# A cast moved from an engine to a DMA transfer in three of 24 groups, with output products one step later

## The chip, the cores and the metric

The kernel runs on one core of a Trainium2 chip. Its time is the device time of one execution in microseconds (us); the number compared is the median of several runs. Five engines work side by side, each through its own queue in order: TensorE (PE in the rows), VectorE (DVE), ScalarE (ACT), GpSimd (POOL) and SyncE (SP), which here issues all transfers between HBM and the on-chip memory SBUF and the transposing transfers inside SBUF. Results of matrix products land in PSUM, which GpSimd and transfers don't use in this kernel.

## The reference

Three steps follow each other. First an attention: `kv` (384 x 32 positions, 128 channels) is averaged over 4 x 4 blocks to 768 keys, multiplied by `w_sr`, and serves as keys and values for 12288 queries:

```python
s = scale * (q @ k.transpose(0, 2, 1))
a = softmax(s)                      # shown in short
x = a @ v
```

Then two layers with 2048 inner features follow, with float64 weights:

```python
h = x @ w_in;  g = maximum(0.01 * h, h);               x = g @ w_out    # first layer
h = x @ w_in;  g = h if h >= 1, 0 if h <= -1, else (h + 1)**2 / 4;  out = g @ w_out
```

## The kernel before

**Groups and steps.** The 12288 tokens are cut into 24 groups of 512 columns. Each layer treats its 2048 inner features in 16 steps of 128. To keep the precision with 16-bit products, each operand is split into a high half and a low half (`..h`, `..l`), and a product of two operands is three matmuls: high by high, low by high, high by low.

**One step of the first layer** (group g, step j). `proj_in` makes three matmuls into a PSUM tile `h`. `leaky` on ScalarE applies the activation and writes `lt` in float32 (line 764). `leaky_hi` makes `gh`, a float16 copy of `lt` (line 772): on ScalarE in group 1 and on GpSimd from group 2 on (`GP = 2`). Group 0 uses float32 products and has no split. `leaky_lo` on VectorE makes `gl = lt - gh` (line 777). `proj_out` adds three matmuls into the accumulator `acc`: part 0 the two on `gh`, part 1 the one on `gl` (line 748). The tile rings hold 6 tiles of `lt` (`LT`) and 6 pairs of `gh` and `gl` (`B0`).

**One step of the second layer.** `quad_a`, `quad_s` (ScalarE), `quad_g` (VectorE), `quad_hi` (ScalarE or, in part from group 4 on, GpSimd) and `quad_lo` (VectorE) do the same for the other activation. The second layer of a group begins well after its first layer: at the start of the kernel several first layers run before any second one, and from some 170 us on the two are interleaved step by step, with the attention of a later group between them.

**Weights and attention.** In the first 100 us the weights are converted as well (lines 346 to 365 and the helpers at lines 115 and 118). The attention of each group makes four tiles of 128 queries, whose 768 weights are normalised on ScalarE and VectorE and transposed by a transfer that SP issues (line 529).

**What sets the order.** Nothing is ordered at run time but by each engine's queue. A planner inside the kernel (`op` and `run_list`) writes these queues. Each operation is entered with a wished-for step number (`when`), an engine, an estimated cost in ns (`cost`), the time after its end until others see it (`late`), the tiles that it needs and makes, and the ring that it takes a slot of. `run_list` then simulates the engines and always emits the operation that can start first, corrected by its wished-for step. Output products of the first layer have the wished-for step `b + F1 + 0.4 * p` with `F1 = 3`, where b is the step of their first products. Operations of VectorE and GpSimd that share a memory port (`port`) exclude each other in the simulation through `lock`, and a GpSimd operation that would have to wait for the lock is put back by 100 ns (line 963).

Of the kernel before, what the change touches and what calls it, by code (L numbers as in the profile page):

```python
# [20 lines left out]
POOL = 4  # L21
# [7 lines left out]
def attention_moe_kernel(  # L29
# [22 lines left out]
    nc = tc.nc  # L52
# [715 lines left out]
    def leaky_hi(g, j):  # L768
        e = st[g][0, j]
        hilo(e, 0, g, j, B0)  # L770
        copy = nc.gpsimd.tensor_copy if g >= GP else nc.scalar.copy
        copy(e["gh"], e["t"])  # L772

# [129 lines left out]
    def op(when, engine, cost, fn, *args, uses=(), makes=(), takes=(), holds=(), late=100):  # L903


        port = (engine == "POOL" and cost > 300) or (
            engine == "DVE"
            and fn in (att_q, att_norm, kv_lo, leaky_lo, quad_s, quad_hi, quad_lo, weight_value, weight_parts)
        )
        todo.append(  # L910
            dict(
                when=when,
                at=len(todo),
                engine=engine,
                cost=cost,
                late=late,
                port=port,
                fn=fn,
                args=args,
                uses=list(uses),  # L920
                makes=list(makes),
                takes=list(takes),
                holds=list(holds),
            )
        )

    def run_list():
# [20 lines left out]
        while any(open_ops.values()):  # L948
            best = {}
            for e, ops in open_ops.items():  # L950
                for o in ops:
                    t = max(free[e], o["ready"])
                    o["slot"] = free[e]
                    for tag, n, x in o["takes"]:
                        ring = tiles.setdefault(tag, [])
                        if len(ring) >= n:
                            late = ((SLOT + 400 * (150000 < t < 1185000)) * (tag != "h") + 300 * (150000 < t < 1185000) * (tag == "h")) * (e == "PE")
                            o["slot"] = max(o["slot"], freed.get(ring[-n], 1e12) + wait[e] + late)
                            t = max(t, o["slot"])
                    turn = 0  # L960
                    if o["port"]:
                        other = lock["POOL" if e == "DVE" else "DVE"]
                        turn = 100 * (e == "POOL" and t < other and t > PATE)
                        t = max(t, other)
                    k = (t + (PAT * min(max(o["when"] + 40, 0), 60) if t < PATE else max(PAT2 * (o["when"] - t / 1300), PATM)), o["when"], o["at"])
                    if e not in best or k < best[e][0]:
                        best[e] = k, t, o, turn
            _, _, t, o = min(((t + turn, k, t, o) for k, t, o, turn in best.values()), key=lambda x: x[:2])
            assert t < 1e12, ("stuck", [(q["when"], q["fn"].__name__, q["args"]) for v in open_ops.values() for q in v][:20])
            e = o["engine"]  # L970
            open_ops[e].remove(o)
            o["start"] = t
            o["idle"] = 0
            if e == "PE" and o["fn"] in FILLED and IDLE0 < t < IDLE1 and o["cost"] > 100:
                o["idle"] = max(0, int((t - o["slot"] - 100) * FF / 56))
            for tag, _, x in o["takes"]:
                tiles[tag].append(x)
            if e == "SP":

                load = o["fn"] in (load_sr, load_q, load_kv, load_weight)  # L980
                free[e] = t + (470 if load else 60)
                begin = max(t + (850 if load else 1300), free["DMA"])
                free["DMA"] = begin + o["cost"]
                end = free["DMA"] + o["late"]
            else:
                free[e] = t + o["cost"]
                end = t + o["cost"] + o["late"]
                if o["port"]:
                    lock[e] = t + o["cost"] - (66 if e == "DVE" or o["fn"] == kv_add else 200)
            o["end"] = end  # L990
            for x in {*o["uses"], *o["makes"], *o["holds"]}:
                if x in held:
                    held[x] -= (x in o["uses"]) + (x in o["makes"]) + (x in o["holds"])
                    o_end = max(freed.get(("part", x), 0), end)
                    freed["part", x] = o_end
                    if not held[x]:
                        freed[x] = o_end
            for w in o.get("then", ()):
                w["left"] -= 1
                same = w["engine"] == e == "PE"  # L1000
                w["ready"] = max(w["ready"], t if same else end + wait[w["engine"]] + (SAFE[e] + 400 * (150000 < end < 1185000)) * (w["engine"] == "PE"))
                if not w["left"]:
                    open_ops[w["engine"]].append(w)
            made.append(o)
# [14 lines left out]
    G16 = 5  # L1019
    QB, B0, B1 = 1, 6, 6  # L1020
    LT, QN, QG = 6, 3, 4
    F1, F2 = 3, 3.8
    FA, FB, FC = 0.5, 0, 3.6
    LAST_HI = ["PPPPPPPPPPPPPPPP", "PPPPPPPPPPPPPPAV"]
    LAST_SQ = ()
    G2, M2 = 4, 2
    CP, TP = 690, 690
    GP = 2
    KEEP, KB = NG, 1
    YB = 6  # L1030
    E0, ES, O0, OS = 13.5, 0.5, 16, 0.5
    PS, KS = 0, 1930
    LG, LM, KL = 1, 1, 1350

    def lo_pool(g, j):
        return g < LG and j % LM == 0
# [32 lines left out]
    def act(n, g):  # L1069
        return n - 365 * (1 - part[g])  # L1070
# [4 lines left out]
    def pool(n, g):  # L1075
        return n - 440 * (1 - part[g])
# [118 lines left out]
    for g in range(NG):  # L1195
# [62 lines left out]
        for m in range(2):  # L1258
            for j in range(NJ):
# [13 lines left out]
                if m == 0:  # L1273
                    op(b + 0.3, "ACT", act(477, g), leaky, g, j, uses=[("h", *h)], makes=[("t", *h)], takes=[("lt", LT, ("t", *h))], late=124)
                    if g < PLAIN:
                        op(
                            b + F0, "PE", pe(870, g), proj_out, 0, g, j, 0,
                            uses=[("t", *h), ("wt2", 0, 1, i), ("wt", 0, 1, i)] + ([("ab", 0, g)] if j else []) + ([("an", 0, g)] if j == NJ - 1 else []),
                            makes=[("acc", 0, g)] + ([] if j else [("ab", 0, g)]) + ([("an", 0, g)] if j < NJ - 1 else []),
                            takes=[] if j else [(("acc", 0), 1, ("accb", 0, g))], late=240,  # L1280
                        )
                        continue
                    e = "POOL" if g >= GP else "ACT"
                    op(b + 0.6, e, pool(CP, g) if e == "POOL" else act(508, g), leaky_hi, g, j, uses=[("t", *h)], makes=[("gh", *h)], takes=[("g0", B0, ("g", *h))], late=-75 if e == "POOL" else 110)
                    e = "POOL" if lo_pool(g, j) else "DVE"
                    op(b + 0.9, e, pool(KL, g) if e == "POOL" else dve(602, g), leaky_lo, g, j, uses=[("t", *h), ("gh", *h)], makes=[("gl", *h)], late=85)
                else:
                    sq = square_engine(g, j)
                    op(b + 0.3, sq, act(662, g) if sq == "ACT" else dve(660, g), quad_a, g, j, uses=[("h", *h), ("units", g), "m2"], makes=[("qa", *h)], takes=[("qa", QN, ("qa", *h))], late=120)
                    op(b + 0.5, sq, act(519, g) if sq == "ACT" else dve(602, g), quad_s, g, j, uses=[("qa", *h)], makes=[("qs", *h)], takes=[("qs", QN, ("qs", *h))], late=123)  # L1290
                    op(b + 0.8, "DVE", dve(658, g), quad_g, g, j, uses=[("qs", *h), ("h", *h), ("units", g)], makes=[("t", *h)], takes=[("qg", QG, ("t", *h))], late=85)
                    if g == NG - 1 and j >= LAST_W:
                        op(
                            b + F2, "PE", pe(870, g), proj_out, m, g, j, 0,
                            uses=[("t", *h), ("whole", i), ("ab", m, g)] + [("an", m, g)] * (j == NJ - 1),
                            makes=[("acc", m, g)] + [("an", m, g)] * (j < NJ - 1), late=240,
                        )
                        continue
                    e = hi_engine(g, j)
                    op(b + 1.1, e, pool(TP, g) if e == "POOL" else act(519, g) if e == "ACT" else 200, quad_hi, g, j, uses=[("t", *h)], makes=[("gh", *h)], takes=[("g1", B1, ("g", *h))], late=-75 if e == "POOL" else 117)  # L1300
                    op(b + 1.5, "DVE", dve(602, g), quad_lo, g, j, uses=[("t", *h), ("gh", *h)], makes=[("gl", *h)], late=85)
# [106 lines left out]
```

## Time and profile before

| | us |
|---|---|
| median of 3 runs (1230.29 to 1230.78) | 1230.58 |
| profiled execution | 1229.88 |
| its span, first to last instruction | 1228.1 |
| TensorE busy | 1215.1 |
| VectorE busy | 1112.6 |
| ScalarE busy | 1092.3 |
| GpSimd busy | 426.9 |

Busy time is the time in which at least one instruction of the engine was in work. Matmuls overlap in TensorE's pipeline, so its busy time contains small holes that don't show. Times within the span count from the first instruction.

### The profile page before, as it was taken

The page shows a single profiled execution, that of the slowest core. Times are in us where ns is not written, and L with a number is a line of the kernel's source. Part 1 is how long each engine was busy: PE and PEld are TensorE (multiplying, and loading weights), DVE is VectorE, ACT ScalarE, POOL GpSimd, SP SyncE. Part 2 cuts the span into 40 slices and gives each one's busy share as a digit, 9 for nine tenths or more (in the row PEclk, how much of TensorE's full clock was granted, in tenths as well). Part 3 has the DMA queues.
Part 4 walks back from the last instruction along what each step waited for, and adds up shares of the span by engine and source line. Part 5 has one row for each costly group of instructions (what it writes and reads, how often), then busy time and mean ns, then how long its engine had stood idle before and what let it go on. Part 6 is the DMA issues. An engine that isn't in the chain of part 4 may idle for free. (4 is left out here: it accounts for less than half of the span.)

```text
span 1228.1 us, 17458 instructions
## 1 busy us (share of the span) xinstructions
PE 1215.1 (99%) x5812; PEld 580.0 (47%) x5812; DVE 1112.6 (91%) x2034; ACT 1092.3 (89%) x1903; POOL 426.9 (35%) x536
## 2 busy tenths in 40 slices
PE   8999999999999999999999999999999999999998
PEld 7544444444444444444444444444444444444443
DVE  6999989989899898989989889898898989989888
ACT  4998889999999898889989889898898988989888
POOL 4004322122143443333433334333443433334454
PEclk9999999999999999999999999999999999999999
DMA  9832222112122121212212112121221211212000
GB/s 355 241 62 39 49 48 53 39 35 48 35 49 43 35 48 44 44 39 44 39 43 57 26 44 49 35 48 35 44 48 35 48 35 26 48 35 39 10 9 18
DMA packets 160218, 65.02 MB, mean 53 GB/s; under 512 B 147072, under 2 KB 151296, under 8 KB 160128
## 3 DMA queue, kind: packets, MB, share of 16 engines
q1 hardware_dynamic: 160128, 63.91, 22.7%
q8 instruction: 45, 0.74, 0.2%
q14 instruction: 45, 0.37, 0.1%
HBM read 21.04 MB, written 6.29 MB: 22 GB/s over the span
## 5 line engine op out<-in xcount | busy, mean ns | idle before, releaser
L772 POOL CAST gh<-lt 128x512 f16<-128x512 f32 x352 | 273.2, 778 | 634.9 <-ACT lt L764 613.5
L801 ACT ACTIVATE qa<-h,yu 128x512 f32<-128x512 f32 x384 | 296.5, 776 | 27.0 <-PE h L731 25.4
L814 DVE SCALAR_TENSOR_TENSOR qg<-qs,yu,h 128x512 f32<-128x512 f32 x384 | 283.6, 739 | 24.5 <-ACT qs L809 22.9
L831 DVE SCALAR_TENSOR_TENSOR gl<-qg,gh 128x512 f16<-128x512 f32 x380 | 271.9, 718 | 23.5 <-ACT gh L827 10.6
L777 DVE TENSOR_TENSOR gl<-lt,gh 128x512 f16<-128x512 f32 x368 | 263.9, 720 | 21.0 <-POOL gh L772 20.0
L809 ACT ACTIVATE qs<-qa 128x512 f32<-128x512 f32 x384 | 241.1, 630 | 4.5
L764 ACT ACTIVATE lt<-h 128x512 f32<-128x512 f32 x384 | 226.1, 593 | 21.4 <-PE h L731 12.2
L823 POOL TENSOR_SCALAR gh<-qg 128x512 f16<-128x512 f32 x154 | 138.7, 900 | 151.0 <-DVE qg L814 95.1
L827 ACT ACTIVATE gh<-qg 128x512 f16<-128x512 f32 x226 | 141.2, 628 | 31.9 <-DVE qg L814 30.3
L731 PE MATMUL h<-yh,w_in1h 128*128 128x512 f16 x384 | 145.6, 379 | 0.9 <-ACT lt L764 0.7
L731 PE MATMUL h<-yh,w_in1l 128*128 128x512 f16 x384 | 145.6, 379 | 0.0
L731 PE MATMUL h<-yl,w_in1h 128*128 128x512 f16 x384 | 145.6, 379 | 0.0
L748 PE MATMUL acc<-gh,w_out1l 128*128 128x512 f16 x380 | 144.1, 379 | 0.0
L748 PE MATMUL acc<-gl,w_out1h 128*128 128x512 f16 x380 | 144.1, 379 | 0.0
L748 PE MATMUL acc<-gh,w_out1h 128*128 128x512 f16 x380 | 144.1, 379 | 0.0
L748 PE MATMUL acc<-gl,w_out0h 128*128 128x512 f16 x368 | 139.4, 379 | 1.6 <-DVE gl L777 1.5
L748 PE MATMUL acc<-gh,w_out0h 128*128 128x512 f16 x368 | 139.6, 379 | 0.3 <-ACT gh L772 0.3
L731 PE MATMUL h<-xh,w_in0h 128*128 128x512 f16 x368 | 139.6, 379 | 0.2
L731 PE MATMUL h<-xl,w_in0h 128*128 128x512 f16 x368 | 139.6, 379 | 0.0
L748 PE MATMUL acc<-gh,w_out0l 128*128 128x512 f16 x368 | 139.6, 379 | 0.0
L731 PE MATMUL h<-xh,w_in0l 128*128 128x512 f16 x368 | 139.6, 379 | 0.0
L731 PEld LDWEIGHTS <-w_in1h 128*128 128x128 f16 x768 | 75.0, 98 | 89.3 <-issue 1.7
(188 smaller groups left out, 1629.5 us busy)
## 6 DMA issues: line engine op xcount, KB each, us to landing
q<-in_q SPq DMA_DIRECT2D x24, 256.0 KB, 2.7
out<-ot SPq DMA_DIRECT2D x24, 256.0 KB, 2.0
kv<-in_kv SPq DMA_DIRECT2D x11, 512.0 KB, 8.6
raw<-in_moe_w_in SPq DMA_DIRECT2D x8, 512.0 KB, 8.2
raw<-in_moe_w_out SPq DMA_DIRECT2D x8, 512.0 KB, 8.6
at<-a SPq DMA_TRANSPOSE x92, 3.7
kv<-in_kv SPq DMA_DIRECT2D x2, 256.0 KB, 10.1
w_sr_sb<-in_w_sr SPq DMA_DIRECT2D x1, 64.0 KB, 1.8
```

Of the source, the lines that this page charges most:

```text
L731: mm(h, w[:, j, :], x, start=(n == 0), stop=(n == 2))
L748: mm(d["acc", m], w_out[m][w][:, j, :], e[x], start=(j == 0 and n == 0), stop=(j == NJ - 1 and n == 2),)
L764: nc.scalar.activation(e["t"], e["h"], AF.Prelu, scale=1.0 if g < PLAIN else 2.0**-15, alpha=SLOPE)
L772: copy(e["gh"], e["t"])
L777: engine.tensor_tensor(e["gl"], e["t"], e["gh"], op=ALU.subtract)
L801: nc.scalar.activation(e["a"], e["h"], AF.Relu, bias=unit(g, 3), scale=unit(g, 2))
L809: nc.scalar.activation(e["s"], e["a"], AF.Square)
L814: nc.vector.scalar_tensor_tensor(e["g"], e["s"], unit(g, 1), e["h"], op0=ALU.min, op1=ALU.max)
L823: nc.gpsimd.tensor_scalar(e["gh"], e["g"], 2.0**-14, 1.0, op0=ALU.mult, op1=ALU.mult)
L827: nc.scalar.activation(e["gh"], e["g"], AF.Copy, scale=2.0**-14)
L831: nc.vector.scalar_tensor_tensor(e["gl"], e["g"], 2.0**-14, e["gh"], op0=ALU.mult, op1=ALU.subtract)
```

## The change

1. In groups 1 to 3 (`by_dma`), `gh` is no longer computed by an engine: GpSimd issues a transfer from `lt` to `gh` inside SBUF, which converts float32 to float16 on its way. Group 1 had its copy on ScalarE, groups 2 and 3 on GpSimd. From group 4 on nothing changes in this operation.
2. The planner enters such a transfer with a cost of 1000 ns on GpSimd and 2000 ns more until it is seen (`CD`, `LD`), and doesn't count it among the operations that use the shared port.
3. Output products of the first layer are wished for 4 steps after their first products, not 3 (`F1`), in all groups.
4. A GpSimd operation that finds the port taken is no longer put back by 100 ns (`TURN = 0`), in the whole plan.

```diff
     def leaky_hi(g, j):
         e = st[g][0, j]
         hilo(e, 0, g, j, B0)
+        if by_dma(g, j):
+            nc.gpsimd.dma_start(e["gh"], e["t"])
+            return
         copy = nc.gpsimd.tensor_copy if g >= GP else nc.scalar.copy
         copy(e["gh"], e["t"])
...
-        port = (engine == "POOL" and cost > 300) or (
+        port = (engine == "POOL" and cost > 300 and not (fn == leaky_hi and by_dma(*args))) or (
...
-                        turn = 100 * (e == "POOL" and t < other and t > PATE)
+                        turn = TURN * (e == "POOL" and t < other and t > PATE)
...
-    F1, F2 = 3, 3.8
+    F1, F2 = 4, 3.8
...
+    GD, GE, CD, LD, TURN = 1, 4, 1000, 2000, 0
...
+    def by_dma(g, j):
+        return GD <= g < GE
...
-                    e = "POOL" if g >= GP else "ACT"
-                    op(b + 0.6, e, pool(CP, g) if e == "POOL" else act(508, g), leaky_hi, g, j, uses=[("t", *h)], makes=[("gh", *h)], takes=[("g0", B0, ("g", *h))], late=-75 if e == "POOL" else 110)
+                    e = "POOL" if g >= GP or by_dma(g, j) else "ACT"
+                    op(
+                        b + 0.6, e, CD if by_dma(g, j) else pool(CP, g) if e == "POOL" else act(508, g), leaky_hi, g, j, uses=[("t", *h)], makes=[("gh", *h)],
+                        takes=[("g0", B0, ("g", *h))], late=LD if by_dma(g, j) else -75 if e == "POOL" else 110,
+                    )
```

## Rows read from the trace of the kernel before

**Rows 1.** The page: span, busy time of each engine, granted clock in 40 slices.

```profile
span 1228.1 us, 17458 instructions
...
PE 1215.1 (99%) x5812; PEld 580.0 (47%) x5812; DVE 1112.6 (91%) x2034; ACT 1092.3 (89%) x1903; POOL 426.9 (35%) x536
...
PEclk9999999999999999999999999999999999999999
```

**Rows 2.** Busy time by stage: stretch, its length, then each engine, clock, DMA.

```profile
72.00:98.00 26.00, 26.00 (x122) 12.78 (x121) 24.31 (x47) 25.65 (x54) 0.00 (x0) 1.00 0.20 42
98.00:126.00 28.00, 26.68 (x125) 13.16 (x123) 27.36 (x55) 24.00 (x44) 14.45 (x24) 1.00 0.22 43
126.00:154.00 28.00, 27.35 (x131) 14.02 (x130) 27.39 (x47) 22.80 (x41) 9.89 (x10) 1.00 0.28 53
...
172.00:1170.00 998.00, 997.09 (x4761) 462.54 (x4760) 908.79 (x1638) 901.79 (x1537) 354.35 (x441) 1.00 0.20 40
```

**Rows 3.** TensorE in order of time around its holes: start, duration, instruction.

```profile
99.67 0.38 PE L748 MATMUL acc<-gl,w_out0h 128*128 128x512 f16 x1
100.33 0.38 PE L748 MATMUL acc<-gh,w_out0h 128*128 128x512 f16 x1 [0.28 <-ACT gh L772]
...
122.26 0.38 PE L748 MATMUL acc<-gh,w_out0l 128*128 128x512 f16 x1
123.21 0.38 PE L748 MATMUL acc<-gl,w_out0h 128*128 128x512 f16 x1 [0.57 <-DVE gl L777]
...
153.46 0.38 PE L731 MATMUL h<-xl,w_in0h 128*128 128x512 f16 x1
153.74 0.38 PE L748 MATMUL acc<-gl,w_out0h 128*128 128x512 f16 x1
```

**Rows 4.** Waits at 70 to 175 us: us in total, times, longest.

```profile
PE acc L748 <- DVE gl L777: 1.5, 3, 0.6
```

**Rows 5.** Groups of instructions at 72 to 172 us; then first-layer tiles at 70 to 101.

```profile
L777 DVE TENSOR_TENSOR gl<-lt,gh 128x512 f16<-128x512 f32 x48 | 35.5, 756 | 1.7 <-POOL gh L772 1.0 <-ACT gh L772 0.6
L772 POOL CAST gh<-lt 128x512 f16<-128x512 f32 x32 | 28.8, 913 | 119.4 <-ACT lt L764 116.9 <-DVE mx L490 1.4 <-ACT keep L841 0.9
...
L772 ACT CAST gh<-lt 128x512 f16<-128x512 f32 x16 | 9.7, 637 | 0.0
...
L764 ACT ACTIVATE lt<-h x18: 576/605/662, 72.3 to 100.7; 128x512 f32<-128x512 f32 x18
L777 DVE TENSOR_TENSOR gl<-lt,gh x16: 681/686/701, 73.9 to 100.3; 128x512 f16<-128x512 f32 x16
```

**Rows 6.** The low half at 180 to 1200 us; Vector's waits for casts after 180 us.

```profile
L777 DVE TENSOR_TENSOR gl<-lt,gh x317: 666/683/1096, 183.6 to 1184.5; 128x512 f16<-128x512 f32 x159
...
DVE gl L777 <- POOL gh L772: 18.2, 39, 1.4
```

**Rows 7.** First-layer tiles at 100 to 125 us, then 138 to 170: shortest/middle/longest, first to last.

```profile
L764 ACT ACTIVATE lt<-h x16: 573/597/627, 100.2 to 123.3; 128x512 f32<-128x512 f32 x16
...
L764 ACT ACTIVATE lt<-h x16: 577/590/607, 138.6 to 168.5; 128x512 f32<-128x512 f32 x16
L772 POOL CAST gh<-lt x16: 613/926/1742, 139.3 to 169.1; 128x512 f16<-128x512 f32 x16
```

**Rows 8.** The stores in the page's list of transfers: count, KB each, middle us to landing.

```profile
out<-ot SPq DMA_DIRECT2D x24, 256.0 KB, 2.0
```

**Rows 9.** Transfers issued at 100 to 172 us; DMA share in 40 slices, GB/s.

```profile
DMA  0002800918200097300190000009009007340000
GB/s 0 0 0 49 169 0 0 186 33 167 52 0 0 0 82 158 133 0 5 27 191 0 5 0 0 0 10 206 6 18 207 7 0 146 73 146 0 0 0 0
...
q<-in_q SPq DMA_DIRECT2D x2, 256.0 KB, 2.8
at<-a SPq DMA_TRANSPOSE x8, 3.7
```

**Rows 10.** Vector's operation on raw weights: shortest/middle/longest ns, first to last start.

```profile
L357 DVE TENSOR_SCALAR raw<-raw x16: 398/421/431, 22.5 to 85.0; 128x512 uint32<-128x512 uint32 x16
```

## The prediction

> **What bounds the kernel now.** I read the page first [rows 1]: TensorE (PE) is busy 1215.1 us of a span of 1228.1, and its granted clock is at full speed in every slice. So the sum of matmul time sets the end, and a change that leaves the matmuls alone can gain only what PE loses in holes. The second view, busy time by stage, says where they are [rows 2]. From 172 to 1170 us PE is idle 0.9 us in 998. The stretch of 98 to 154 us, where groups 2 and 3 go through the first layer, has holes: 26.68 of 28 and 27.35 of 28. Vector is at 27.36 and 27.39 of 28 there.
>
> A row's PE time hides part of a hole: a matmul of 512 columns shows 0.38 us, yet the next one starts 0.215 us later when nothing holds it. So I take holes from start to start, less 0.215 [rows 3]. At 123.21: 123.21 - 122.26 - 0.215 = 0.735. Nine such holes lie in front of output products of the first layer, the first (0.445) at 100.33 and the last (0.065) at 153.74; between them 0.155 at 112.62, 0.255 at 114.48, 0.06 at 117.88, 0.495 at 121.18, 0.735 at 123.21, 0.175 at 125.76 and 0.765 at 149.79. The nine make 3.15 us. Two more (104.94, 107.47; 0.185 each) stand in front of first products, which the change doesn't serve directly. The view of waits names the cause of the three largest as Vector's low half, `gl` [rows 4].
>
> Why is `gl` late? In 72 to 172 us it takes 0.756 us in the mean [rows 5], in the steady part 0.683 in the middle [rows 6]; the longest take 1.09. GpSimd's cast, which makes its input `gh`, takes 0.61 us at the least, 0.913 in the mean of these 32 and 1.74 at the longest [rows 5, 7]. The two stretch each other, and Vector has no spare time there.
>
> **The change part by part.** Matmuls: none added, none removed.
>
> *The high half of groups 2 and 3.* 32 casts of 0.913 leave GpSimd (28.8 us, off the path). Vector's `gl` no longer runs beside a cast: the first 16 (group 1, cast on ScalarE) took 0.69, so the other 32 took (35.5 - 16 x 0.69) / 32 = 0.76, and they fall to 0.683. That is 32 x 0.08 = 2.5 us of Vector's time in a stretch of 74 us. The 3.15 us of holes are due to late `gl`, and with more distance between `gh` and its use they can close whole.
>
> *The high half of group 1.* 16 casts of 0.637 (9.7 us) leave ScalarE, which is 25.65 of 26 busy at 72 to 98 us [rows 2, 5]. PE is busy 26.00 of 26 there, so this gains nothing; it can only lose, if the transfer is late.
>
> *The transfer's price.* The trace of before has no transfer from GpSimd, so its time from issue to landing, L, is bounded. Each moves 256 KB in and half of that out. The issue: between 0 and 1.74, the longest cast on that engine [rows 7]. The moving: between 2.0 (a 256 KB store) and 3.7 (a transpose) [rows 8, 9]; no load larger than 256 KB is issued in 100 to 172 us. So L lies between 2.0 and 5.4. I take 0.61 for the issue (an undisturbed cast) and 2.8 for the moving (the q loads of that stretch, of equal size [rows 9]): L = 3.4. The plan in the code counts 1.0 + 2.0.
>
> *What hides it.* The output products now trail by 4 steps, the one on `gl` by 4.4. A step is (123.3 - 100.2) / 15 = 1.54 us in group 2, (100.7 - 72.3) / 17 = 1.67 in group 1, (168.5 - 138.6) / 15 = 1.99 in group 3 [rows 5, 7]. In 4.4 steps of group 2, 6.78 us, must fit: three first products 0.65, `lt` 0.59, L, one Vector instruction ahead 0.72, `gl` 0.69, and some 0.3 for four handovers: 2.95 + L. So L is hidden up to 3.8 us in group 2, 4.4 in group 1, 5.8 in group 3. L = 3.4 fits. If that cover is gone, the wait falls on Vector first, whose queue is in order: behind a late `gl` stand the attention's maxima and normalising operations and the second layer's `qg` and `gl`, and behind those PE.
>
> *Other traffic.* Eight transposes start in 100 to 172 us, each 3.7 us to landing, holding nine tenths of the DMA engines at the peaks [rows 9]. A cast that meets one shares the engines; 256 KB at the 207 GB/s of the peaks are 1.3 us, so sharing makes L about 4.7, 0.9 over the cover of group 2. Being late once shifts all that follows alike, so I charge it once, at even odds: 0.45 us. The transposes and SP's queue have no wait on the casts. GpSimd's queue holds next to nothing but these transfers between 72 and 172 us, so a transfer waiting for its buffer blocks nothing else.
>
> *Buffers.* `gh` and `gl` have 6 each. Held from issue to the last product they need 6.78 - 1.24 + 0.4 = 5.9 us, 3.9 steps of group 2. `lt` is held 0.59 + 3.4 + 0.72 + 0.69 = 5.4 us, 3.5 of 6. No new wait.
>
> *The later groups.* F1 = 4 and the new tie rule (TURN = 0) reorder the 317 casts after 180 us too. PE's 0.9 us of idleness there is all that can be gained; I count 0, with bounds of -0.9 and +6.6 (below).
>
> **The sum.** 1229.88 us is the profiled execution, 1228.1 of it span. 1229.88 - 3.15 + 0.45 = 1227.2. The median of the runs is 0.70 above that execution, so 1227.9.
>
> **The rivals.** *B: the holes stay in part.* Vector remains full (27.4 of 28), so `gl` is late for its queue, not for its input, or L is 4.4: then group 2 runs at (2.95 + 4.4) / 4.4 = 1.67 a step, 16 x 0.13 = 2.1 us longer. 1230.58 - 3.15 + 2.1 = 1229.5. For it: Vector's busy share, and that the smaller holes show no wait in the trace. Against: the largest holes name `gl` while casts beside it are stretched.
>
> *C, slower: the transfer is longer than its cover.* At L = 5.4 the in-order loop from first product to output product takes (2.95 + 5.4) / 4.4 = 1.90 us a step. Group 2 loses 16 x 0.36 = 5.7 us, group 1 16 x 0.23 = 3.7, group 3 nothing: 1230.58 - 3.15 + 9.4 = 1236.8. It decides from L = 4.6 on, where the loss (16 x 0.18 + 16 x 0.05 = 3.6) passes the gain. For it: the casts' stretch to 1.74 beside Vector may hold for descriptor writing as well, and transposes share the engines. Against: the 256 KB loads of that stretch land in 2.8 us [rows 9].
>
> One row bears on C in particular. A Vector operation on raw weights handles 512 columns in 0.42 us where `gl` needs 0.68, so it runs at more than one column a cycle; 16 of them run, the last at 85.0 us [rows 10], so few can meet the transfers. The Trainium skill (SBUF — State Buffer, "Who interferes with whom") says that such faster Vector forms shut GpSimd out of writing descriptors for the whole instruction, and that forms with two SBUF inputs disturb only what GpSimd reads. By that rule transfers after 85 us aren't stretched, and C would shrink; no run here shows it yet.
>
> *D, slower: the reordering costs in the steady part.* Vector already waits 18.2 us, 39 times, for casts after 180 us [rows 6]. If casts and Vector's work now collide so that PE waits once in every second group for 0.66 us (the mean of the three largest holes), ten waits cost 6.6: 1230.58 - 2.7 + 6.6 = 1234.5. Against: PE's idle time there is next to nothing, and one step more of distance helps.
>
> **How the numbers follow.** Forecast 0.50, B 0.24, C 0.17, D 0.09. About 0.2% (2.46 us) is what a measurement of this kernel tells from no change: faster is below 1228.1, slower above 1233.0. The forecast's own range is 1225.8 (all eleven holes and the later 0.9 us closed, nothing paid) to 1229.0; 0.08 of its 0.50 is "same". So faster 0.42, same 0.08 + 0.24 = 0.32, slower 0.26. The range takes in B, D's value and the milder half of C: 1225.5 to 1235.0.
>
> **What would show it.** Right: PE near 28 of 28 in 98 to 154 us, no wait of PE on `gl` or `gh`, `gl` near 0.69, casts from issue to landing under 3.8 us. C: landing above 4.6 us, Vector idle before `gl` with the DMA as releaser, first-layer steps of 1.7 us and more. B: shorter `gl` with the holes still there. D: new PE waits after 172 us. The forecast is wrong if the span isn't shorter though the holes are gone, for then PE lost as much elsewhere.

## The result, and the profile after

The changed kernel takes 1240.95 us (median of six runs, 1240.57 to 1242.69), the kernel before 1230.57 beside it: 10.4 us slower, ratio 1.0088 with a 95% interval of 1.0075 to 1.0101. The forecast was 1227.9, the range ended at 1235.0. The profiled execution of the kernel after is the one at 1240.95; its span is 1239.1 us.

From the page of the kernel after: span, busy time, the new transfer queue (packets, MB, share of the 16 DMA engines) and the transfers (count, KB, middle us to landing). The first two answer to [rows 1].

```profile
span 1239.1 us, 17486 instructions
...
PE 1216.4 (98%) x5812; PEld 579.7 (47%) x5812; DVE 1102.1 (89%) x2034; ACT 1082.3 (87%) x1887; POOL 424.6 (34%) x552
...
q0 software_dynamic: 6912, 6.29, 3.4%
...
gh<-lt POOLq DMA_DIRECT2D x48, 128.0 KB, 2.7
```

TensorE has the same 5812 matmuls, and the span is 11 us longer: the time is in holes. Vector and ScalarE are each some 10 us less busy, so neither became the bound by having more to do.

Busy time by stage of the kernel after, columns as in [rows 2]:

```profile
72.00:98.00 26.00, 24.67 (x113) 11.65 (x112) 24.06 (x47) 20.19 (x42) 8.56 (x15) 1.00 0.70 112
98.00:126.00 28.00, 26.31 (x127) 13.76 (x126) 24.83 (x56) 20.74 (x37) 8.81 (x25) 1.00 0.73 110
126.00:154.00 28.00, 24.23 (x111) 11.50 (x111) 19.57 (x38) 20.95 (x38) 4.20 (x8) 1.00 0.66 94
154.00:182.00 28.00, 26.19 (x124) 12.19 (x123) 22.09 (x40) 18.81 (x32) 5.36 (x10) 1.00 0.55 89
...
172.00:1170.00 998.00, 995.52 (x4752) 462.05 (x4751) 904.18 (x1637) 895.85 (x1531) 350.80 (x436) 1.00 0.20 41
```

The stretch of 154 to 182 us in the kernel before:

```profile
154.00:182.00 28.00, 28.00 (x136) 13.00 (x135) 24.19 (x44) 23.92 (x41) 6.99 (x10) 1.00 0.25 52
```

Three stretches answer for the loss, and the long steady part with them. TensorE was without a hole at 72 to 98 us and lacks 1.33 us now; at 126 to 154 it lacks 3.77 instead of 0.65; at 154 to 182, with the later steps of group 3, it lacks 1.81 instead of nothing. And from 172 to 1170 us it lacks 2.48 us instead of 0.91. The DMA engines' share at 98 to 126 us went from 0.22 to 0.73.

Waits at 72 to 182 us of the kernel after (us in total, times, longest), which answer to [rows 4]:

```profile
DVE gl L780 <- DMA gh<-lt: 9.7, 7, 3.0
PE acc L748 <- DMA gh<-lt: 4.5, 5, 1.7
PE ya L867 <- DVE ytop L861: 1.4, 1, 1.4
PE xp L697 <- DMA at<-a: 0.7, 1, 0.7
```

Vector waits 9.7 us for the transfers, TensorE 4.5 us itself, and 1.4 us more for an operation of Vector that stood behind such a wait.

The tile `gh` at 70 to 180 us (shortest/middle/longest ns of the issue and of the low half, which answer to [rows 5, 7]), and the time from issue to landing in three stretches: the whole, 147.9 to 153 and 122.9 to 126.5 us:

```profile
L772 POOL DMA_DIRECT2D gh<-lt x48: 527/527/990, 73.8 to 177.3; - x48
L780 DVE TENSOR_TENSOR gl<-lt,gh x47: 665/683/693, 76.8 to 175.2; 128x512 f16<-128x512 f32 x47
...
DMA to landing us min/median/max: 2.3/2.7/8.3
...
DMA to landing us min/median/max: 2.3/2.3/3.0
...
DMA to landing us min/median/max: 5.0/5.4/8.3
```

At 147.9 to 153 us, where nothing else of SP's is under way, the transfers land in 2.3 to 3.0 us though they follow each other closely; the forecast had 3.4. One that is issued at 122.9 to 126.5 us needs 5.0 to 8.3. What it meets there is the attention's traffic, which SP issued just before:

```profile
122.06 1.49 SPq L529 DMA_TRANSPOSE at<-a  x1
123.64 1.12 SPq L127 DMA_DIRECT2D q<-in_q  x1
125.47 3.60 SPq L529 DMA_TRANSPOSE at<-a  x1
```

Of the 48 transfers 14 take over 4 us, all of them beside a transpose or a q load; the mean of all is 3.35. All transfers at 72 to 172 us, first of the kernel after, then of the one before (compare [rows 9], which begin at 100):

```profile
gh<-lt POOLq DMA_DIRECT2D x47, 128.0 KB, 2.7
q<-in_q SPq DMA_DIRECT2D x3, 256.0 KB, 4.6
at<-a SPq DMA_TRANSPOSE x10, 5.0
```

```profile
q<-in_q SPq DMA_DIRECT2D x3, 256.0 KB, 2.8
at<-a SPq DMA_TRANSPOSE x10, 3.7
```

The delay is mutual: transposes take 5.0 us instead of 3.7, loads of q 4.6 instead of 2.8.

The kernel after in order of time at 126 to 135 us (start, duration, instruction, idle time before it):

```profile
126.55 0.39 PE L748 MATMUL acc<-gl,w_out0h 128*128 128x512 f16 x1
128.12 0.69 DVE L780 TENSOR_TENSOR gl<-lt,gh 128x512 f16<-128x512 f32 x1 [2.08 <-DMA gh<-lt]
128.13 0.38 PE L748 MATMUL acc<-gh,w_out0h 128*128 128x512 f16 x1 [1.20 <-DMA gh<-lt]
...
128.73 0.95 DVE L490 TENSOR_REDUCE mx<-s 128x1 f32<-128x768 f32 x1
...
129.71 0.90 ACT L495 ACTIVATE a<-s,mx 128x768 f32<-128x768 f32 x1 [3.85 <-DVE mx L490]
...
134.51 0.69 DVE L780 TENSOR_TENSOR gl<-lt,gh 128x512 f16<-128x512 f32 x1 [3.00 <-DMA gh<-lt]
134.53 0.38 PE L748 MATMUL acc<-gh,w_out0h 128*128 128x512 f16 x1 [1.74 <-DMA gh<-lt]
...
135.31 0.93 ACT L115 ACTIVATE a<-a,sm 128x768 f16<-128x768 f32 x1 [3.28 <-DVE sm L510]
```

This is how one late transfer spreads. Vector stands 2.08 us before `gl`; the attention's maximum behind it in the queue starts late; ScalarE, which needs the maximum, stands 3.85 us. TensorE itself stands 1.2 us for the same transfer. At 134.5 it repeats.

**Holes as in [rows 3].** Start to start, less the pace of the matmul before, without holes under 25 ns and without the second products of the attention scores (which show gaps of a like size in every kernel):

| kernel | holes at 72 to 182 us | after 182 us |
|---|---|---|
| before | 3.7 | 2.8 |
| after | 11.8 | 5.0 |

The difference is 8.1 + 2.2 = 10.3 us; the two spans differ by 11.0, and some 0.5 us of that lies before 72 us, where no cast has yet become a transfer. The first number is for the transfers to explain, the second for the new order.

### The profile page after: what moved, and what is told of

It reads as the page before. It is cut to its first block, busy times and chain, and to the rows that moved or that the text cites. A ratio compares the mean times of both kernels' runs of the same rounds, so it can differ in the third digit from the quotient of the medians.

```text
span 1239.1 us, 17486 instructions
## 1 busy us (share of the span) xinstructions
PE 1216.4 (98%) x5812; PEld 579.7 (47%) x5812; DVE 1102.1 (89%) x2034; ACT 1082.3 (87%) x1887; POOL 424.6 (34%) x552
## 5 line engine op out<-in xcount | busy, mean ns | idle before, releaser
L775 POOL CAST gh<-lt 128x512 f16<-128x512 f32 x320 | 244.0, 764 | 510.6 <-ACT lt L764 484.1
L780 DVE TENSOR_TENSOR gl<-lt,gh 128x512 f16<-128x512 f32 x368 | 258.1, 705 | 37.7 <-POOL gh L775 24.3
L834 DVE SCALAR_TENSOR_TENSOR gl<-qg,gh 128x512 f16<-128x512 f32 x380 | 267.0, 704 | 20.0 <-POOL gh L826 11.3
## 6 DMA issues: line engine op xcount, KB each, us to landing
kv<-in_kv SPq DMA_DIRECT2D x2, 256.0 KB, 10.3
```

What stands on the lines that cost most here:

```text
L780: engine.tensor_tensor(e["gl"], e["t"], e["gh"], op=ALU.subtract)
L834: nc.vector.scalar_tensor_tensor(e["gl"], e["g"], 2.0**-14, e["gh"], op0=ALU.mult, op1=ALU.subtract)
```

## The experiments

Each kernel was timed in five rounds beside the kernel before; ratios with 95% intervals are to that kernel. In the table trail is `F1` in steps, ties is `TURN` in ns, and planned 4.5 late means `LD = 4500` on top of the cost of 1000. The times are medians in us; the holes are those of the one profiled execution. In two of these, of the trail alone (1237.50) and the ties alone (1232.08), TensorE loses some 2 us more than in the kernel before already ahead of 72 us, so they lie above their medians; the holes in the table don't contain this.

| kernel | time | ratio (interval) | holes 72 to 182 | after 182 |
|---|---|---|---|---|
| no transfer, trail 4, ties 0 | 1233.17 | 1.0021 (1.0012 to 1.0030) | 3.8 | 5.6 |
| transfer, trail 3, ties 100 | 1234.58 | 1.0032 (1.0019 to 1.0045) | 7.2 | 3.1 |
| after, plain copies for transposes | 1236.24 | 1.0048 (1.0035 to 1.0060) | 7.9 | 5.2 |
| after, planned 4.5 late | 1231.36 | 1.0008 (1.0000 to 1.0017) | 2.6 | 5.1 |
| after, planned 3.0 late | 1234.41 | 1.0033 (1.0020 to 1.0045) | 4.7 | 5.4 |
| planned 4.5 late, trail 3, ties 100 | 1230.15 | 1.0003 (0.9994 to 1.0012) | 3.1 | 2.7 |
| the same, groups 2 and 3 alone | 1231.24 | 1.0009 (1.0000 to 1.0017) | 4.6 | 2.7 |
| trail 4 alone | 1236.67 | 1.0050 (1.0036 to 1.0064) | 4.0 | 7.6 |
| ties 0 alone | 1230.70 | 1.0000 (0.9991 to 1.0009) | 4.1 | 2.5 |
| transfers and transposes planned late | 1230.32 | 1.0000 (0.9991 to 1.0009) | 4.0 | 2.5 |
| the same, ties 0 | 1230.50 | 1.0001 (0.9993 to 1.0010) | 3.5 | 2.4 |
| trail 4 alone, 7 pairs | 1235.93 | 1.0041 (1.0028 to 1.0055) | 4.9 | 6.8 |

**No transfer.** Is it the transfers or the order?

```diff
-    GD, GE, CD, LD, TURN = 1, 4, 1000, 2000, 0
+    GD, GE, CD, LD, TURN = 0, 0, 1000, 2000, 0
```

> The changed kernel with no transfer at all: the high half is made by ScalarE in group 1 and by GpSimd from group 2 on, as before; the four-step trail and the new tie rule stay. Theory T (the transfers are late where they meet other traffic, and that costs some 9 us of the 10.4): 1229 to 1232.5, with the holes of 72 to 178 us down to 2 to 4 us in all and, after 180 us, still some 2 us more than before if the new order has a price there. Rival D (the new order of the whole plan is what costs): 1237 or more.

1233.17: 0.7 us above the upper end given by the theory of late transfers, and far from D's 1237. The new order costs 2.8 us, all of it after 182 us; the transfers in that order cost 1240.95 - 1233.17 = 7.8 us.

**The transfer alone**, with the old trail and tie rule.

```diff
-    F1, F2 = 4, 3.8
+    F1, F2 = 3, 3.8
...
-    GD, GE, CD, LD, TURN = 1, 4, 1000, 2000, 0
+    GD, GE, CD, LD, TURN = 1, 4, 1000, 2000, 100
```

> The transfers alone: groups 1 to 3 by transfer as in the changed kernel, but output products trail by three steps and a GpSimd operation that finds the port taken is put back by 100 ns, as before. Theory T: 1238 to 1243, as slow as the changed kernel or slower, since the plan has less distance to cover a late transfer; holes after 180 us as in the kernel before. Rival D: within 3 us of the kernel before.

1234.58, below the 1238 that I had expected at the least and above D's 3 us: in the old order the transfers cost 4.2 us, not 7.8. The waits are of the same kind; at 72 to 182 us:

```profile
DVE gl L780 <- DMA gh<-lt: 8.3, 9, 2.4
PE acc L748 <- DMA gh<-lt: 4.2, 5, 1.4
```

TensorE's own waits for the transfers are nearly those of the changed kernel (4.2 and 4.5 us), but it doesn't wait for `ytop` here. That the price depends on what the order puts behind the waiting instruction fits this; the longest landing is shorter here too, though (5.4 against 8.3 us), so it isn't shown. And a trail of three steps did not make it dearer, which already speaks against the trail as the cover.

**Plain copies in place of transposes.** The attention weights of groups 2 to 4 stay untransposed, so the result differs.

```diff
+            to = d["at"][:, :, :, t * P : (t + 1) * P].rearrange("p n k t -> p (n k) t")
+            if 2 <= g <= 4:
+                nc.sync.dma_start(to, a16.rearrange("p n b (k t) -> p (n b k) t", t=P))
+                return
+            nc.sync.dma_start_transpose(to, a16.rearrange("p n b k -> p (n b k)"))
```

> The changed kernel, in which the attention's transposing transfers of groups 2 to 4 are plain copies of the same bytes (256-byte pieces) by the same queue: the attention weights of these groups stay untransposed, so that part of the result is left out. Theory T in its narrow form (transposes stop the casting transfers as no plain copy does): no transfer from lt to gh takes over 5 us from issue to landing, and 1232 to 1236. Theory T in its wide form (any traffic of that size shares the engines, packet by packet): the landing times stay as they are, up to 5.5 us and more, and 1239 to 1243. Rival D: 1240 to 1242, whatever the landing times.

1236.24, between both forms. Landing goes up to 6.0 us still, and the waits fall without going away; at 72 to 182 us:

```profile
DVE gl L781 <- DMA gh<-lt: 5.7, 7, 2.6
PE acc L749 <- DMA gh<-lt: 3.3, 2, 1.7
```

Plain copies delay the transfers too: 6 of 48 take over 5 us, against 7 beside transposes, and only the longest is clearly shorter (6.0 against 8.3). The profiled execution has a second effect: busy time by stage shows a granted clock (third column from the end) of 0.75 and 0.82 in eight microseconds.

```profile
126.00:130.00 4.00, 3.05 (x9) 1.09 (x9) 2.83 (x5) 1.14 (x3) 0.00 (x0) 0.75 1.00 189
130.00:134.00 4.00, 4.00 (x18) 2.44 (x17) 2.88 (x5) 3.41 (x6) 0.00 (x0) 0.82 0.01 3
```

TensorE had idled 0.95 us in the first stretch and 0.90 of the 4 us before it, and its clock was at the lower of its two levels, 1.2 GHz, for part of both; that is (0.25 + 0.18) x 4 = 1.7 us of clock in this execution, which took 1237.18. The median is free of it: the three executions with a mean granted clock of 1.000 took 1235.80 to 1236.24. How much belongs to transposing and how much to the number of bytes stays open.

**The changed kernel with the transfer planned later.** The cost in the plan alone is changed; the transfers stay as they are.

```diff
-    GD, GE, CD, LD, TURN = 1, 4, 1000, 2000, 0
+    GD, GE, CD, LD, TURN = 1, 4, 1000, 4500, 0
```

> The changed kernel with the transfer planned as seen 4.5 us after its issue is done, not 2.0, so that the order of Vector and TensorE expects it late. Theory T: the holes in front of output products and the waits of Vector on transfers shrink to under a third (below 2 us and 3.5 us), and the time falls to 1231 to 1237; what is left comes from the buffers and from work that is done later. Rival D: 1239 to 1242, since the rest of the order is as in the changed kernel.

1231.36, 1.0 us above the kernel before beside it, where the changed kernel lost 10.4; the theory holds. On the whole the transfers land no faster: the middle one takes 3.0 us (2.7 in the changed kernel), 15 take over 4 us (14), and only the longest is shorter (6.0 against 8.3). At 72 to 182 us there is no wait for them, neither Vector's nor TensorE's; busy time and TensorE's one wait for a transfer:

```profile
72.00:182.00 110.00, 107.80 (x514) 53.39 (x513) 97.98 (x193) 90.17 (x163) 28.68 (x60) 1.00 0.66 105
```

```profile
PE xp L697 <- DMA at<-a: 2.1, 1, 2.1
```

By stage:

```profile
72.00:98.00 26.00, 23.93 (x111) 11.41 (x110) 24.22 (x47) 20.40 (x41) 8.66 (x16) 1.00 0.74 113
98.00:126.00 28.00, 28.00 (x140) 15.06 (x139) 25.83 (x58) 22.29 (x40) 8.77 (x24) 1.00 0.80 136
126.00:154.00 28.00, 28.00 (x136) 14.18 (x135) 25.21 (x52) 25.84 (x47) 5.77 (x11) 1.00 0.65 109
```

So what the forecast wanted at 98 to 154 us is there: TensorE is at 28.00 of 28 twice. It is paid for elsewhere. At 72 to 98 us 2.07 us are lost, nearly all in one hole, an attention product that waits for a transpose which the transfers delay; after 182 us the order with the trail of four costs 2.3 us of holes. Compared with no transfer in the same order, the transfers now gain 1.8 us by the medians, with intervals that just overlap.

**Planned 3.0 late**, the dose between.

```diff
+    GD, GE, CD, LD, TURN = 1, 4, 1000, 3000, 0
```

> The changed kernel with the transfer planned as seen 3.0 us after its issue is done: half way, by effect, between 2.0 (the changed kernel, 11.8 us of holes at 72 to 182 us) and 4.5 (2.6 us). Theory T (the loss is the time by which a transfer outlasts its plan): holes between, 4 to 9 us, and 1233 to 1238. Rival (the order with 4.5 happened to come out well): holes outside of 2.6 to 11.8, or the time outside of 1231.4 to 1241.

1234.41 with 4.7 us of holes: between, as the theory has it. With 2.0, 3.0 and 4.5 the holes are 11.8, 4.7 and 2.6. Quicker transfers are not the reason: here 12 of 48 take over 5 us, in the changed kernel 7.

**The honest plan (4.5 late) in the old order**, without the new trail and tie rule; then in groups 2 and 3 alone (`GD = 2`).

```diff
+    F1, F2 = 3, 3.8
...
+    GD, GE, CD, LD, TURN = 1, 4, 1000, 4500, 100
```

> Groups 1 to 3 by transfer, planned as seen 4.5 us after its issue is done, but with the trail of three steps and the 100 ns as before: only the transfers and an honest plan of them. Theory T2 (two prices that add: a transfer planned too early makes the order wait, and the new trail and tie rule cost 2 to 3 us after 180 us): holes of 72 to 180 us about 2.5 us, one of them in front of an attention product, those after 180 us as before; 1228 to 1230. Rival (the four-step trail is needed to cover a transfer): waits on transfers come back in 72 to 180 us, 1231 or more.

> As the kernel with the honest plan and the old trail and tie rule, but by transfer in groups 2 and 3 alone; group 1 keeps its copy on ScalarE. Theory T2 with its part on group 1 (its transfers serve no hole and only delay the transposes and output products at 72 to 98 us): no hole of over 0.5 us at 72 to 98 us, holes of 72 to 180 us under 1.5 us, 1226.5 to 1228.5, faster than with group 1. Rival (ScalarE's 10 us in group 1 are what pays): 1229 or more, slower than with group 1.

1230.15: no difference from the kernel before, and just outside the 1228 to 1230 expected. No trail of four steps is needed: TensorE waits for no cast, and Vector once, 0.6 us, though 10 of the 48 transfers take over 5 us. But what the nine holes of [rows 3] cost is now lost in others; TensorE's waits at 72 to 182 us:

```profile
PE xp L697 <- DMA at<-a: 1.6, 1, 1.6
PE ya L867 <- DVE qg L817: 0.7, 1, 0.7
```

Without transfers in group 1 it was to be faster and is not: 1231.24. The hole at 72 to 98 us is gone, but others at 98 to 182 us (4.6 us) replace it. My part on group 1 held at 72 to 98 us and fell for the whole; the two times (1231.24 and 1230.15) are not clear of noise from each other, their intervals overlap. That ScalarE's 10 us in group 1 pay is compatible with it, but the reordered plan can explain it as well.

**Transposes of groups 2 to 4 planned later too**, with the old tie rule and without.

```diff
-op(b, "SP", 500, att_norm, g, t, 2, uses=[("a16", g, t)], makes=[("at", g)], late=1900)
+op(b, "SP", 500, att_norm, g, t, 2, uses=[("a16", g, t)], makes=[("at", g)], late=1900 + 2500 * (2 <= g <= 4))
```

> Transfers in groups 1 to 3 planned 4.5 us late, three steps, 100 ns, and the transposes of groups 2 to 4 planned 2.5 us later too, since transfers and transposes delay each other. Theory T: the hole of 1.8 us in front of the first attention product (waiting for a transpose) goes; holes of 72 to 182 us 0.5 to 1.5 us, those after 182 us as before (2.7); 1228 to 1229.3, faster than the kernel before by 1 to 2.5 us. Rival (holes only move, because Vector and ScalarE are full until 130 us): holes of 72 to 182 us stay at 3 us or more, 1229.8 to 1232.

> As the kernel with both planned late, but the GpSimd operation that finds the port taken isn't put back. Theory T with the tie rule alone costing nothing: within 1.5 us of the kernel with both planned late, 1227.5 to 1230. Rival (tie rule and transfers together cost): 1231 or more.

1230.32 and 1230.50: both the same as before. In the first the rival holds: the hole of 1.8 us went, and 4.0 us stand elsewhere, among them a transfer that needed longer than even 4.5. The second lies within 1.5 us of the first, as expected of a tie rule that costs nothing, but above its range. No version here beats the kernel before.

**The order's two parts, each alone, without transfers.**

```diff
+    F1, F2 = 4, 3.8
...
+    GD, GE, CD, LD, TURN = 0, 0, 1000, 2000, 100
```

```diff
+    F1, F2 = 3, 3.8
...
+    GD, GE, CD, LD, TURN = 0, 0, 1000, 2000, 0
```

> No transfer, output products of the first layer trail by four steps, the 100 ns as before. If the trail is what costs in the new order: 1232 to 1234, with the holes after 400 us of 4 to 5 us as in the kernel with both and no transfer. If the tie rule costs: 1229.5 to 1231.

> No transfer, three steps, but a GpSimd operation that finds the port taken isn't put back (0 instead of 100 ns). If the tie rule is what costs in the new order: 1232 to 1234, with holes after 400 us of 4 to 5 us. If the trail costs: 1229.5 to 1231.

The trail is the cost: 1236.67, more than the 1234 expected, while the tie rule alone is neutral (1230.70). Both together are at 1233.17, so the tie rule gives back about half of what the trail costs. It isn't the luck of one plan: after 182 us all seven kernels of this document with a trail of four have 5.0 to 7.6 us of holes, all seven with three have 2.4 to 3.1. Busy time at 182 to 1170 us of the trail alone:

```profile
182.00:1170.00 988.00, 983.98 (x4692) 456.55 (x4691) 897.06 (x1619) 888.02 (x1514) 345.45 (x434) 1.00 0.20 41
```

TensorE idles 4.0 us there, against 0.9 of 988 in the kernel before.

**The trail with 7 pairs of halves.** Does it cost because the ring of `gh` and `gl` runs short?

```diff
-    QB, B0, B1 = 1, 6, 6
+    QB, B0, B1 = 1, 7, 6
```

> The four-step trail alone (no transfer, 100 ns as before), with 7 pairs of the first layer's high and low halves, not 6. If the trail costs because a pair is held a step longer and the ring runs short: the holes after 182 us fall from the 7.6 us of the trail with 6 pairs to 3 us or less, and the time from 1236.7 to 1229.5 to 1232. If it costs because each step's order on the engines comes out worse: holes of 5 us or more and 1234 to 1238.

1235.93 with 6.8 us of holes, 0.8 less than with 6 pairs: the ring is at most a small part of it. TensorE's waits after 182 us in this kernel are in front of first products:

```profile
PE h L731 <- DVE qg L817: 1.8, 6, 0.5
PE h L731 <- ACT lt L764: 1.2, 3, 0.6
PE h L731 <- DVE sm L508: 0.6, 1, 0.6
```

First products wait until ScalarE or Vector has read an older `h` tile. That this comes from more of them standing in a row in the new order is my reading, not shown.

## Why the prediction was wrong

The forecast, faster by 2.7 us at 0.50, fell; what came is rival C with a share of D, and both were priced apart, not together. C's price was not what came either: it had a loop slower at every step of groups 1 and 2 and nothing in group 3, while the runs show single long stops, and group 3 loses 1.81 us at 154 to 182.

*What bounds the kernel, and where the gain can be.* Right. The time moved with TensorE's holes: 10.3 us of holes for spans that differ by 11.0. The nine holes of 3.15 us could be closed, as the kernel with the transfer planned 4.5 late shows at 98 to 154 us. That all nine are due to late `gl` was more than the rows say: three of them, 2.0 us, name it [rows 4], and the one at 100.33 waits for `gh` [rows 3].

*`gl` is late because casts stretch it.* Right as to the stretch: `gl` fell from 0.756 [rows 5] to 0.683 in the mean beside the transfers. In the changed kernel that was worth nothing by itself.

*The transfer's price, L = 3.4.* Too high for a quiet moment (2.3, the issue 0.53) and too low for a busy one (5.0 to 8.3 at 122.9 to 126.5 us). The mean of 3.35 us is nearly the forecast's value; the spread is what it left out.

*Other traffic, 0.45 us: the first step that failed.* I had charged a transfer that meets a transpose 1.3 us by sharing bandwidth, once. It is delayed by up to 6 us (8.3 against 2.3), the transposes and q loads in turn by 1.3 and 1.8, and it repeats, in five places of the changed kernel. "Being late once shifts all that follows alike" was wrong: the order holds pieces that do not depend on the cast, and each of them is made late anew, as the stretch at 126 to 135 us shows.

*What hides it, four steps: the second step that failed, and the larger one.* I took the trail of 4.4 steps for the cover, 3.8 us in group 2. The trail is a wish; where Vector's `gl` stands in its queue follows from the time at which the plan expects `gh`, 1.0 + 2.0 = 3.0 us after the issue begins. With the same trail and 1.0 + 4.5 us in the plan the waits vanish, and with the old trail all but one of 0.6 us. The prediction had that number in hand ("The plan in the code counts 1.0 + 2.0") and didn't use it. The diff said so: `late=LD` is what the plan computes with. That the wait falls on Vector first, with the attention's maxima and the second layer behind it, was as written.

*Group 1 can only lose.* Right at 72 to 98 us: 1.33 us are lost there in the kernel as changed, 2.07 in the same order planned 4.5 late, none with transfers in groups 2 and 3 alone. Over the whole kernel the run without group 1 was not faster (1231.24 against 1230.15), so what group 1 is worth there stays open.

*The later groups, 0 us with bounds of -0.9 and +6.6.* The value failed, the bounds held: +2.8 with both parts, +6.1 with the trail alone. "One step more of distance helps" was wrong.

*The range.* Its lower end doesn't come out of its own terms: 1230.58 - 3.15 - 0.37 - 0.9 is 1226.2, not 1225.8. Nothing hangs on it.

*The fast Vector form.* The Trainium skill (SBUF — State Buffer, "Who interferes with whom") says that Vector's two-port forms keep GpSimd from writing descriptors. The traces agree in part. 46 of the 48 issues take 0.53 us beside a Vector engine that is nearly always busy, the first 0.76, and the longest, 0.99 us, spans the last two operations on raw weights. But with plain copies for transposes an issue beside the same two operations takes 0.53. GpSimd's and Vector's rows of the kernel after, then of the one with plain copies (two issues and two operations merged each time):

```profile
87.16 1.51 POOL L772 DMA_DIRECT2D gh<-lt  x2 [3.01 <-ACT lt L764]
...
87.28 0.75 DVE L357 TENSOR_SCALAR raw<-raw 128x512 uint32<-128x512 uint32 x2
```

```profile
86.84 1.18 POOL L773 DMA_DIRECT2D gh<-lt  x2 [3.04 <-ACT lt L765]
...
86.79 0.82 DVE L357 TENSOR_SCALAR raw<-raw 128x512 uint32<-128x512 uint32 x2
```

It costs one issue 0.46 us at the most; it is not why the transfers are late.

**What stays open.** How one of these orders could keep the gain of 98 to 154 us without paying for it at 72 to 98 or after 182; why transfers cost 7.8 us in the new order and 4.2 in the old; by what the DMA engines let a transpose delay a cast so much more than its bytes take; and why the trail of four steps orders the steady part worse.

## What to carry to other kernels

Where a planner writes the queues, an operation's cost in the plan is part of the change: a cast that lands in 2.3 us alone and in 5 to 8 beside transposes has to be planned near its late value, or every in-order queue that takes it stands. The value to plan with is the late one, not the mean (3.35 us here). Distance wished for is not distance given; look for the number from which the position is computed. And in a kernel whose bound engine is 99% busy, price a global reordering by trying it alone: here it cost as much as the whole gain in sight.

## What the runs showed of the hardware that I had not expected

A transfer issued by GpSimd, 256 KB of float32 into 128 KB of float16 inside SBUF, costs that engine 0.53 us and lands after 2.3 us when nothing else moves, less than a load of 256 KB from HBM (2.8). Beside transposes the bytes moved no longer explain the time. The kernel after at 130 to 132 us, in which the DMA engines count as busy more than once over while hardly anything moves (the last two columns: share of the engines, GB/s):

```profile
130.00:131.00 1.00, 0.61 (x4) 0.21 (x3) 0.52 (x2) 1.00 (x3) 0.00 (x0) 1.00 1.95 82
131.00:132.00 1.00, 1.00 (x8) 0.69 (x6) 0.52 (x2) 0.97 (x2) 0.00 (x0) 1.00 1.28 30
```

Packets of casts and transposes are open there at the same time, single ones for 1.5 us and more. A 16 KB fetch of instructions falls in the same two microseconds; whether it adds to this was not tried, but it can't be the cause everywhere: beside the transpose of 78.45 us, where casts take up to 5.2 us, no instructions are fetched.
